# Transposing a per-pair attention tile by DMA instead of on TensorE, with the add on VectorE and a longer lag of the MLP

## The chip, the cores and the metric

One Trainium2 chip, one core. The metric is device time in microseconds (us) of one execution. The kernel before takes 316 to 318 us. One slot below means one step of the main loop: one head's scores for 128 keys. A pair is two heads and has 12 slots; a batch is four pairs and has 48 slots.

## The reference

```python
# q, k, v: [4, 8, 768, 64]; block-sparse mask over 24 blocks of 32
scores = q @ k.T / 8, masked; attn = softmax(scores); x = attn @ v     # -> x: [4, 768, 512]
xt = x.transpose(0, 2, 1)
h  = xt @ U @ V                              # low-rank mixer over the sequence, rank 32
u  = x + h.transpose(0, 2, 1)
out = u + relu(u @ w_ch1) @ w_ch2            # 512 -> 2048 -> 512
```

## The kernel before

For every pair of heads the kernel computes 12 score tiles (two matmuls of 384 columns each), takes their exponentials on ScalarE, multiplies them with v (`av`), casts the normalized result to fp16 (`xh`), and forms `uT`, the transposed input of the MLP: x transposed plus the mixer's product. The MLP of a batch runs as 56 steps (32 for the first layer, 24 for the second), which are dealt out over the slots of the next batch, so that TensorE always has work while ScalarE takes exponentials.

In the kernel before, `xh` is transposed on TensorE: six matmuls against the identity, accumulated in PSUM with the mixer product, and then one cast to SBUF by VectorE.

```python
    def ut(c):                                   # c = 0, 1: two halves of the sequence
        pu = psa([P, HS], FP32)                  # one of two PSUM buffers "pa"
        for j in range(3):
            nc.tensor.matmul(pu[:, j * P : (j + 1) * P], xh[:, 3 * c + j, :], id16,
                             start=(j == 0), stop=False, ...)
        nc.tensor.matmul(pu, bt.a16[:, ch], Vt[...], start=False, stop=True, ...)
        nc.vector.tensor_copy(out=bt.uT[hp][:, c * HS : (c + 1) * HS], in_=pu)

    return {1: [lambda: av(0)], 3: [lambda: av(1)], 5: [mix],
            6: [lambda: ut(0)], 7: [lambda: ut(1)]}   # slots after the pair's last score
```

q, k and v are loaded by DMA from the queue of SyncE (SP), cast by GpSimd into `qst` and `kst`, and, from pair 6 on, transposed by DMAs from the same queue that transpose on the way (crossbar DMA). Two staging buffers each are reused by every other pair. The w2 weights are loaded from GpSimd's queue near 51 us.

```python
    def load_qk(i): ...   # nc.sync.dma_start(ld <- q, k); nc.gpsimd.tensor_copy(qst[i % 2] <- ld)
    def front(i):   ...   # i >= 6: nc.sync.dma_start_transpose(aq <- qst), (ak <- kst)

    for i in range(NPAIR):
        if i + 2 < NPAIR:
            last = load_qk(i + 2)
            load_v(i + 2)
            ...
        if i + 1 < NPAIR and i + 1 >= NPE:
            front(i + 1)
        ...           # 12 slots: scores, delayed functions of the pair before, MLP steps
```

The softmax here doesn't subtract the row's maximum and nothing guards it: scores larger than these inputs give would overflow.

Of the kernel before, what the change touches and what calls it, by code (L numbers as in the profile page):

```python
# [10 lines left out]
FP16 = mybir.dt.float16  # L11
# [3 lines left out]
ALU = mybir.AluOpType  # L15

P = 128
# [3 lines left out]
def kernel(  # L21
# [14 lines left out]
    nc = tc.nc  # L36

    B, H, S, D = q.shape
    BLK = 32
    NB = S // BLK  # L40
    T = S // P
    HD = H * D
    HP = H // 2
# [4 lines left out]
    HS = S // 2  # L48
# [31 lines left out]
    wpool = ctx.enter_context(tc.tile_pool(name="wpool", bufs=1))  # L80
    ldpool = ctx.enter_context(tc.tile_pool(name="ldpool", bufs=2))
    augp = ctx.enter_context(tc.tile_pool(name="augp", bufs=3))
    epool = ctx.enter_context(tc.tile_pool(name="epool", bufs=20))
    xpool = ctx.enter_context(tc.tile_pool(name="xpool", bufs=2))
    upool = ctx.enter_context(tc.tile_pool(name="upool", bufs=2))
    tpool = ctx.enter_context(tc.tile_pool(name="tpool", bufs=18))
# [13 lines left out]
    def psa(shape, dtype):  # L100
        return psap.tile(shape, dtype, tag="pa", name="pa")
# [5 lines left out]
    id16 = eye[:, 0:P]  # L107
# [14 lines left out]
    def load_qk(i):  # L122
        b, hp = divmod(i, HP)
        last = None
        for src, st, nm in ((q, qst, "qld"), (k, kst, "kld")):
            ld = ldpool.tile([P, 2, T, D], FP32, tag="ld" + nm, name=nm)
            nc.sync.dma_start(
                out=ld,
                in_=src[b, 2 * hp : 2 * hp + 2].rearrange("h (p t) d -> p h t d", t=T),
            )  # L130
            dst = st[i % NST][:, :, :, 0:D]
            last = nc.gpsimd.tensor_copy(out=dst, in_=ld)  # L132
        return last

    def load_v(i):
        b, hp = divmod(i, HP)
        ld = ldpool.tile([P, 2, T, D], FP32, tag="ldv", name="vld")
        nc.sync.dma_start(
            out=ld,
            in_=v[b, 2 * hp : 2 * hp + 2].rearrange("h (p t) d -> p h t d", t=T),  # L140
        )
        nc.gpsimd.tensor_copy(out=vts[b % 2][:, 2 * hp : 2 * hp + 2, :, 0:D], in_=ld)
# [3 lines left out]
        out=sb[0:NB].rearrange("k z r w -> k (z r w)"),  # L146
        in_=sampled_blocks.bitcast(I32).rearrange("z r -> (z r)")[None, :].broadcast_to(
            [NB, NB * 6]
        ),
# [3 lines left out]
    for h, eng in ((0, nc.sync), (1, nc.sync)):  # L153
        for src, nm in ((q, "qld"), (k, "kld")):
            if h == 0:
                lds[nm] = ldpool.tile([P, 2, T, D], FP32, tag="ld" + nm, name=nm)
            eng.dma_start(  # L157
                out=lds[nm][:, h], in_=src[0, h].rearrange("(p t) d -> p t d", t=T)
# [22 lines left out]
    for r in range(3):  # L181
        nc.vector.scalar_tensor_tensor(
            out=a01[0:NB], in0=sb[0:NB, :, r, 0], scalar=iota,
            in1=prev, op0=ALU.is_equal, op1=ALU.max,
# [3 lines left out]
        out=bias[0:NB, 0:NB], in0=a01[0:NB],  # L188
# [3 lines left out]
    for t in range(T):  # L192
        nc.tensor.matmul(
            pb[:, t, :], ohT[:, t * P : (t + 1) * P], bias[0:NB, :],
            start=True, stop=True,
# [10 lines left out]
    def load_mix():  # L206
        uld = ldpool.tile([P, T, R], FP32, tag="ldu", name="uld", bufs=1)
        nc.sync.dma_start(out=uld, in_=moe_U.rearrange("(p t) r -> p t r", t=T))
        vld = ldpool.tile([P, S], FP32, tag="ldvv", name="vvld", bufs=1)
        nc.sync.dma_start(out=vld[0:R, :], in_=moe_V)  # L210
        nc.gpsimd.tensor_copy(out=Ut[:, :, 0:R], in_=uld)
        nc.gpsimd.tensor_copy(
            out=Vt[0:R, :, :], in_=vld[0:R, :].rearrange("r (p t) -> r t p", t=T)
        )

    def load_w1(cs):
        for cc in cs:
            nc.gpsimd.dma_start(
                out=w1t[:, cc, :], in_=moe_w_ch1[cc * P : (cc + 1) * P, :]
            )  # L220

    def load_w2(js):
        for j in js:
            nc.gpsimd.dma_start(
                out=w2t[:, j : j + 4, :],
                in_=moe_w_ch2[j * P : (j + 4) * P, :].rearrange(
                    "(j p) d -> p j d", p=P
                ),
            )
# [3 lines left out]
    NPAIR = B * HP  # L233
# [51 lines left out]
    def pair_tail(i, bt, ests):  # L285
        b, hp = divmod(i, HP)
        vt = vts[b % 2]
        xh = xpool.tile([P, T, P], FP16, tag="xh", name="xh", bufs=3)
        ch = slice(hp * P, (hp + 1) * P)

        def av(c):
            pav = psa([P, 3, 2, D + 1], FP32)
            for h in range(2):
                for j in range(3):
                    sc = 3 * c + j
                    for g in range(T):
                        nc.tensor.matmul(  # L297
                            pav[:, j, h, :],
                            ests[h][g][:, sc * P : (sc + 1) * P],
                            vt[:, 2 * hp + h, g, 0 : D + 1],  # L300
                            start=(g == 0), stop=(g == T - 1),
                        )
            rcp = misc.tile([P, 3, 2], FP32, tag="rcp", name="rcp")
            nc.vector.reciprocal(out=rcp, in_=pav[:, :, :, D])  # L304
            xs = bt.xf[:, 3 * c : 3 * c + 3, ch]
            nc.vector.tensor_tensor(  # L306
                out=xs.rearrange("p j (h d) -> p j h d", h=2),
                in0=pav[:, :, :, 0:D],
                in1=rcp[:, :, :, None].broadcast_to([P, 3, 2, D]),
                op=ALU.mult,  # L310
            )
            nc.vector.tensor_copy(out=xh[:, 3 * c : 3 * c + 3, :], in_=xs)  # L312

        def mix():
            pa = psa([P, P], FP32)
            for sc in range(T):
                nc.tensor.matmul(  # L317
                    pa, Ut[:, sc, :], xh[:, sc, :], start=(sc == 0), stop=(sc == T - 1)
                )
            nc.vector.tensor_copy(out=bt.a16[:, ch], in_=pa)  # L320

        def ut(c):
            pu = psa([P, HS], FP32)
            for j in range(3):
                nc.tensor.matmul(  # L325
                    pu[:, j * P : (j + 1) * P], xh[:, 3 * c + j, :], id16,
                    start=(j == 0), stop=False, skip_group_check=True,
                )
            nc.tensor.matmul(  # L329
                pu,  # L330
                bt.a16[:, ch],
                Vt[:, 3 * c : 3 * c + 3, :].rearrange("r t p -> r (t p)"),
                start=False, stop=True, skip_group_check=True,
            )
            nc.vector.tensor_copy(out=bt.uT[hp][:, c * HS : (c + 1) * HS], in_=pu)

        return {
            1: [lambda: av(0)],
            3: [lambda: av(1)],
            5: [mix],  # L340
            6: [lambda: ut(0)],
            7: [lambda: ut(1)],
        }

# [50 lines left out]



    LAG = 8
    SLOTS = HP * 2 * T
    queue = []  # L400
    delayed = {}
    arrivals = {}
    slot = 0

    def run_delayed():
        for fn in delayed.pop(slot, ()):
            fn()
        queue.extend(arrivals.pop(slot, ()))
# [5 lines left out]
    for i in range(NPAIR):  # L414
        b, hp = divmod(i, HP)
        if hp == 0:
            bt = Batch()
            done, due = 0.0, 0.0
# [3 lines that stand above are left out]
            if i == 0:  # L422
                load_mix()
            with tc.issue_after(last.ins):
                if i == 0:
                    load_w1((0, 1))
                elif i == 1:
                    load_w1((2, 3))
                elif i == 4:
                    load_w2((0, 4, 8, 12))  # L430
        if i + 1 < NPAIR and i + 1 >= NPE:
            front(i + 1)
        ests = [[], []]
        for h in range(2):
            for g in range(T):
                ests[h].append(scores(i, h, g))
                run_delayed()
                n = slot % SLOTS
                if b > 0:
                    left = SLOTS - n  # L440
                    rest = [c for c, _ in queue]
                    if arrivals:
                        rest += [c for c, _ in arrivals_all]
                    keep = LAG if b + 1 < B else 0
                    due += sum(rest[: len(rest) - keep]) / left
                    while queue and done + queue[0][0] / 2 <= due:
                        c, fn = queue.pop(0)
                        fn()
                        done += c
                if i + 1 < NPE and (h, g) == (1, 2):  # L450
                    front(i + 1)
                slot += 1
        for d, fns in pair_tail(i, bt, ests).items():
            delayed.setdefault(slot + d, []).extend(fns)
        if hp == HP - 1:
            arrivals_all = mlp_steps(b, bt)
            arrivals[slot + 8] = arrivals_all
    while delayed:
        run_delayed()
        if queue:  # L460
# [37 lines left out]
```

## Time and profile before

The lines are from the page of the kernel before: busy time of each engine, then, for 40 equal slices of the span (7.9 us each), the busy share of TensorE, the clock granted to it and the busy share of the DMA engines, in tenths.

```profile
PE 304.8 (97%) x2840; PEld 188.6 (60%) x2840; DVE 128.6 (41%) x265; ACT 179.7 (57%) x261; POOL 48.0 (15%) x66
...
PE   6899999999999999999999999999999999999994
...
PEclk9999999999999999999999999999999999999999
DMA  7999887999797873551406160160001001000111
```

TensorE is busy from end to end at full clock. DMA is busy for seven tenths of the time or more in each of the first 15 slices, that is for batch 0 and most of batch 1 (to about 118 us), and less after that. The chain of work that ended last says the same:

```profile
PE 86%; ACT 7%; DMA 2%; DVE 1%; issue 1%; POOL 1%; SPq 1%; ACTq 0%
```

The groups of instructions (busy us, mean ns of one) show the identity matmuls, and a VectorE operation of the kind that the change adds:

```profile
L325 PE MATMUL pa<-eye,xh 128*128 128x128 f16 x96 | 10.6, 219 | 0.0
L306 DVE TENSOR_TENSOR xf<-pa,rcp 128x384 f32<-128x384 f32 x32 | 17.8, 557 | 1.1
```

The 219 ns is the modelled duration of one matmul, which overlaps its neighbours. What one costs is seen from start times in the timeline (start us, modelled duration, instruction, how many):

```profile
140.10 0.33 PE L325 MATMUL pa<-eye,xh 128*128 128x128 f16 x3
140.26 0.33 PE L329 MATMUL pa<-Vt,a_1986 128*128 128x384 f16 x1
140.43 0.33 PE L354 MATMUL pm<-uT_951,w1t 128*128 128x384 f16 x1
```

Three identity matmuls take from 140.10 to 140.26 us, 54 ns each. The queue of SP, again as a timeline, shows what a crossbar transpose (of q or k, twice the size of xh) costs to issue, once while DMA is full and once while it is not:

```profile
55.76 5.94 SPq L251 DMA_TRANSPOSE aq<-qst_99  x1
61.76 7.94 SPq L251 DMA_TRANSPOSE ak<-kst_101  x1
...
129.56 1.42 SPq L251 DMA_TRANSPOSE aq<-qst_100  x1
131.03 1.83 SPq L251 DMA_TRANSPOSE ak<-kst_102  x1
```

### The profile page before, as it was taken

How to read it: one execution, taken by the hardware profiler on the slowest of the kernel's cores; microseconds unless marked ns; L12 is line 12 of the kernel's file. 1: busy time of each engine (PE TensorE's matmuls, PEld its weight loads, DVE VectorE, ACT ScalarE, POOL GpSimd, SP SyncE). 2: the span in 40 equal slices, each digit the busy share in tenths (PEclk: the TensorE clock that was granted, in tenths of full speed). 3: DMA queues.
4: the chain of work that ended last, by engine and by line, in shares of the span. 5: the costliest groups of instructions: out<-in, count | busy, mean ns of one | idle time of the engine just before them, and what ended most of it. 6: DMA issues, size and time to landing. Idle time of an engine off the chain costs nothing.

```text
span 314.6 us, 6818 instructions
## 1 busy us (share of the span) xinstructions
PE 304.8 (97%) x2840; PEld 188.6 (60%) x2840; DVE 128.6 (41%) x265; ACT 179.7 (57%) x261; POOL 48.0 (15%) x66
## 2 busy tenths in 40 slices
PE   6899999999999999999999999999999999999994
PEld 3577666676756555666756555576665656565441
DVE  3455566545342424453533423454441334543111
ACT  4799988477756554767664554766655352332000
POOL 3871357004212311010202000000000000000000
PEclk9999999999999999999999999999999999999999
DMA  7999887999797873551406160160001001000111
GB/s 222 344 293 247 310 245 207 216 182 192 194 202 204 237 150 130 112 124 31 71 2 135 52 150 36 50 85 2 0 2 67 35 35 68 2 0 1 69 67 67
DMA packets 51031, 38.05 MB, mean 121 GB/s; under 512 B 32744, under 2 KB 47384, under 8 KB 51000
## 3 DMA queue, kind: packets, MB, share of 16 engines
q1 hardware_dynamic: 48240, 33.37, 40.3%
q0 software_dynamic: 2688, 4.19, 7.4%
q8 instruction: 22, 0.36, 0.5%
q14 instruction: 9, 0.07, 0.1%
q10 hardware_dynamic: 72, 0.05, 0.1%
HBM read 27.64 MB, written 6.29 MB: 108 GB/s over the span
## 4 chain that ended last, share of the span: by engine, by line
PE 86%; ACT 7%; DMA 2%; DVE 1%; issue 1%; POOL 1%; SPq 1%; ACTq 0%
PE pm L373 23%; PE pm L354 23%; PE psc L262 17%; PE pa L297 9%; ACT est L268 7%; PE pa L354 3%; PE pa L373 3%; PE pa L317 2%; DMA vld<-in_v_dram 2%; PE pa L329 2%; PE pm L371 1%; PE pa L325 1%; PE pa L245 1%; SPq L157 1%; DVE xf L306 0%
## 5 line engine op out<-in xcount | busy, mean ns | idle before, releaser
L268 ACT ACTIVATE est<-psc 128x768 f16<-128x768 f32 x192 | 150.7, 811 | 68.8 <-PE psc L262 68.1
L262 PE MATMUL psc<-aq,ak 128*128 128x384 f16 x384 | 93.5, 325 | 0.8 <-ACT est L268 0.2
L373 PE MATMUL pm<-w2t,tT 128*128 128x512 f16 x336 | 84.2, 379 | 0.0
L354 PEld LDWEIGHTS <-w1t 128*128 128x128 f16 x512 | 49.0, 98 | 31.0 <-issue 1.4
L373 PEld LDWEIGHTS <-tT 128*128 128x128 f16 x384 | 36.6, 98 | 36.2
L262 PEld LDWEIGHTS <-ak 128*128 128x128 f16 x384 | 36.6, 98 | 28.6 <-issue 1.8
L362 ACT ACTIVATE tT<-pm 128x384 f16<-128x384 f32 x64 | 31.3, 489 | 35.7 <-PE pm L354 19.7
L297 PEld LDWEIGHTS <-est 128*128 128x128 f16 x1152 | 43.0, 97 | 6.6
L364 DVE TENSOR_SCALAR tT<-pm 128x384 f16<-128x384 f32 x48 | 26.8, 557 | 33.4 <-PE pm L354 32.0
L381 DVE TENSOR_TENSOR of<-xf,pm 128x512 f32<-128x512 f32 x21 | 14.4, 685 | 34.1 <-PE pm L373 34.1
L304 DVE RECIPROCAL rcp<-pa 128x6 f32<-128x6 f32 x32 | 6.3, 195 | 52.6 <-PE pa L297 52.6
L297 PE MATMUL pa<-vt_97,est 128*128 128x65 f16 x576 | 24.0, 193 | 0.0
L297 PE MATMUL pa<-vt_98,est 128*128 128x65 f16 x576 | 20.7, 193 | 0.0
L306 DVE TENSOR_TENSOR xf<-pa,rcp 128x384 f32<-128x384 f32 x32 | 17.8, 557 | 1.1
L312 DVE CAST xh<-xf 128x384 f16<-128x384 f32 x32 | 17.6, 551 | 0.9
L364 DVE TENSOR_SCALAR tT<-pa 128x384 f16<-128x384 f32 x16 | 8.9, 557 | 11.3 <-PE pa L354 11.3
L132 POOL CAST qst_100<-qld 128x768 f16<-128x768 f32 x8 | 6.6, 828 | 41.5 <-DMA aq<-qst_100 34.7
L132 POOL CAST qst_99<-qld 128x768 f16<-128x768 f32 x7 | 5.8, 828 | 44.9 <-DMA aq<-qst_99 44.6
L373 PE MATMUL pa<-w2t,tT 128*128 128x512 f16 x48 | 10.8, 379 | 0.0
L325 PE MATMUL pa<-eye,xh 128*128 128x128 f16 x96 | 10.6, 219 | 0.0
L354 PE MATMUL pm<-uT_213,w1t 128*128 128x384 f16 x32 | 10.4, 325 | 0.1
L354 PE MATMUL pm<-uT_1987,w1t 128*128 128x384 f16 x32 | 10.4, 326 | 0.1
(101 smaller groups left out, 304.5 us busy)
## 6 DMA issues: line engine op xcount, KB each, us to landing
vld<-in_v_dram SPq DMA_DIRECT2D x16, 384.0 KB, 4.5
out_dram<-of SPq DMA_DIRECT2D x24, 256.0 KB, 2.0
qld<-in_q_dram SPq DMA_DIRECT2D x15, 384.0 KB, 3.4
kld<-in_k_dram SPq DMA_DIRECT2D x15, 384.0 KB, 6.2
w1t<-in_moe_w_ch_dram POOLq DMA_DIRECT2D x4, 512.0 KB, 8.7
w2t<-in_moe_w_ch_dram POOLq DMA_DIRECT2D x4, 512.0 KB, 13.3
qld<-in_q_dram SPq DMA_DIRECT2D x2, 192.0 KB, 3.4
kld<-in_k_dram SPq DMA_DIRECT2D x2, 192.0 KB, 3.5
```

Of the source, the lines that this page charges most:

```text
L132: last = nc.gpsimd.tensor_copy(out=dst, in_=ld)
L262: nc.tensor.matmul(psc[:, c, 0:HS], kT[:, h, g * P : (g + 1) * P], qT[:, h, c * HS : (c + 1) * HS], start=True, stop=True,)
L268: nc.scalar.activation(out=est.rearrange("k (c n) -> k c n", c=2), in_=psc[:, :, 0:HS], func=AF.Exp, scale=0.125,)
L297: nc.tensor.matmul(pav[:, j, h, :], ests[h][g][:, sc * P : (sc + 1) * P], vt[:, 2 * hp + h, g, 0 : D + 1], start=(g == 0), stop=(g == T - 1),)
L306: nc.vector.tensor_tensor(out=xs.rearrange("p j (h d) -> p j h d", h=2), in0=pav[:, :, :, 0:D], in1=rcp[:, :, :, None].broadcast_to([P, 3, ...
L312: nc.vector.tensor_copy(out=xh[:, 3 * c : 3 * c + 3, :], in_=xs)
L325: nc.tensor.matmul(pu[:, j * P : (j + 1) * P], xh[:, 3 * c + j, :], id16, start=(j == 0), stop=False, skip_group_check=True,)
L354: nc.tensor.matmul(pt, w1t[:, cc, jj * P : (jj + 1) * P], bt.uT[cc][:, c * HS : (c + 1) * HS], start=(cc == 0), stop=(cc == NCC - 1),)
L362: nc.scalar.activation(out=dst, in_=pt, func=AF.Relu)
L364: nc.vector.tensor_scalar_max(out=dst, in0=pt, scalar1=0.0)
L373: nc.tensor.matmul(hold[sc], bt.tT[jj][:, sc * P : (sc + 1) * P], w2t[:, jj, :], start=False, stop=(jj == NJJ - 1),)
L381: nc.vector.tensor_add(out=of, in0=bt.xf[:, sc, :], in1=hold[sc])
```

## The change

For pairs 4 to 14 the six identity matmuls go. `xh` is transposed into a new tile `xT` by a crossbar DMA that is issued from SP after the second attention product, and VectorE adds it to the mixer product in place of the cast. The additions move from slots 6 and 7 to slots 8 and 9 to give the DMA time. The MLP of batches 1 and 2 therefore starts at slot 10 rather than 8, and four more steps of the MLP before it are kept back to fill those slots. The pool of exponentials shrinks from 20 to 18 buffers to make room for `xT`.

```diff
-    epool = ctx.enter_context(tc.tile_pool(name="epool", bufs=20))
+    epool = ctx.enter_context(tc.tile_pool(name="epool", bufs=18))
...
+        xbar = HP <= i < NPAIR - 1
+        xT = xpool.tile([P, T, P], FP16, tag="xT", name="xT") if xbar else None
+
+        def turn():
+            nc.sync.dma_start_transpose(xT, xh.rearrange("p t c -> p (t c)"))
+
         def ut(c):
             pu = psa([P, HS], FP32)
-            for j in range(3):
+            if not xbar:                      # the same three matmuls
...
-            nc.vector.tensor_copy(out=bt.uT[hp][:, c * HS : (c + 1) * HS], in_=pu)
+            if xbar:
+                nc.vector.tensor_tensor(out=dst, in0=pu, in1=xT[...], op=ALU.add)
+            else:
+                nc.vector.tensor_copy(out=dst, in_=pu)
+
+        if xbar:
+            return {
+                1: [lambda: av(0)],
+                3: [lambda: av(1), turn],
+                5: [mix],
+                8: [lambda: ut(0)],
+                9: [lambda: ut(1)],
+            }
...
-    LAG = 8
+    LAG = 12
...
-            arrivals[slot + 8] = arrivals_all
+            arrivals[slot + (10 if 0 < b < B - 1 else 8)] = arrivals_all
```

More of the change, by code (lines that the diff above doesn't have):

```diff
@@ L320, in mix @@
             nc.vector.tensor_copy(out=bt.a16[:, ch], in_=pa)
+        xbar = HP <= i < NPAIR - 1
+        xT = xpool.tile([P, T, P], FP16, tag="xT", name="xT") if xbar else None
+        def turn():
+            nc.sync.dma_start_transpose(xT, xh.rearrange("p t c -> p (t c)"))
         def ut(c):
             pu = psa([P, HS], FP32)
-            for j in range(3):
-                nc.tensor.matmul(
-                    pu[:, j * P : (j + 1) * P], xh[:, 3 * c + j, :], id16,
-                    start=(j == 0), stop=False, skip_group_check=True,
-                )
+            if not xbar:
+                for j in range(3):
+                    nc.tensor.matmul(
+                        pu[:, j * P : (j + 1) * P], xh[:, 3 * c + j, :], id16,
+                        start=(j == 0), stop=False, skip_group_check=True,
+                    )
             nc.tensor.matmul(
@@ L332, in ut @@
                 Vt[:, 3 * c : 3 * c + 3, :].rearrange("r t p -> r (t p)"),
-                start=False, stop=True, skip_group_check=True,
+                start=xbar, stop=True, skip_group_check=True,
             )
-            nc.vector.tensor_copy(out=bt.uT[hp][:, c * HS : (c + 1) * HS], in_=pu)
+            dst = bt.uT[hp][:, c * HS : (c + 1) * HS]
+            if xbar:
+                nc.vector.tensor_tensor(
+                    out=dst, in0=pu,
+                    in1=xT[:, 3 * c : 3 * c + 3, :].rearrange("c t p -> c (t p)"),
+                    op=ALU.add,
+                )
+            else:
[8 more added lines that the diff above has]
+            }
         return {
```

## The prediction

> **What bounds the kernel.** TensorE. The page gives PE 97% busy; busy can hide slack, since ends are modelled, so I took start times from the timeline. From 54 us to the end (ScalarE paces the earlier part) matmuls start back to back: 163 ns per 384 columns, 216 ns per 512, 54 ns per 128, 32 ns per 65. Starts minus these sums leave under 0.5 us per 10 us, except about 1.5 us near 265 us. The granted clock is 1.00. In the chain of waits PE is 86%. VectorE (41%) and ScalarE (57%) have room.
>
> **Removed.** Eleven pairs (4 to 14) each lose six 128-column matmuls, the transposes of xh by the identity: 66 of 96. The group list says 219 ns each and 10.6 us busy for all 96, but neither is the cost: in the timeline three run from 140.10 to 140.26 us, 54 ns each. The Trainium skill ("TensorE: Matmul & The Clock Gate", Part 4) gives about 275 to 390 ns for a PE transpose; that is latency, and this trace's pipelined 54 ns decides. 66 x 54 ns = 3.6 us, all in PE-bound stages, so all on the chain.
>
> **Added.** (a) On VectorE, an add of PSUM and fp16 SBUF for a cast: the cast takes 558 ns, tensor-tensor operations of the same 128x384 shape 557 ns. Free. (b) Eleven crossbar transposes of 128x768 fp16. Those of q and k are twice as large: 1.4 us of issue on SP, 3.8 us at least and 4.7 us in the median to landing, 15.1 us at worst. Estimate for half: 0.7 us issue, about 3 us landing. (c) The addition comes five slots (about 7 us) after the second attention product; xT is ready 1.3 us plus landing after it. Enough where DMA is free (after 125 us: 10 to 40% busy), tight from 54 to 125 us, where DMA is 88% busy. Pair 5 is worst: its xh is cast at 88 us, while SP issues q/k transposes until 92 us. If the new one queues behind them, VectorE waits perhaps 3 us in order; with two PSUM buffers for the MLP some of that reaches PE. I charge 0.5 to 1 us in all.
>
> **Moved.** Twelve lagged steps in place of eight carry four w2 steps (0.86 us each) out of batch 1's stage into later ones. PE is saturated in all, so this saves nothing; it bridges the two slots by which the next MLP starts later (ten slots at about 2100 columns against twelve steps of 2048: no gap). Exponential buffers 20 to 18: never the releaser of a long wait; no effect expected.
>
> **Prediction.** 316.7 - 3.6 + 0.6 = 313.7 us, range 311.6 to 316.6. Faster by over 2%: 0.04; within 2%: 0.92; slower by over 2%: 0.04.
>
> **What would show it right or wrong.** Identity matmuls on xh fall from 96 to 30. Start spacing of other matmuls from 54 us on is unchanged. The uT additions take 0.55 to 0.6 us. VectorE waits for the xT DMA at most once or twice, near 75 to 97 us, and PE shows gaps only there. The stage up to 54 us and the tail from about 263 us keep their lengths.
>
> **What would make it wrong.** If xT lands late in most pairs, in-order VectorE holds both PSUM pools and TensorE stalls: each 1 us late, times eleven, would eat the gain. If the extra DMA delays q/k loads in batch 1's stage, scores start late. If the buffer count reorders the first stage, up to 1 us either way. More than 4 us gained would mean that weight loads or PSUM waits cost more than the timeline's spacing shows.

## The result, and the profile after

The changed kernel takes 330.41 us (median of four runs, 328.92 to 331.66) against 317.48 us. It is slower: the ratio is 1.0409, with a 95% interval of 1.0338 to 1.0479. The prediction said 313.7 us.

The lines of the page of the changed kernel that answer to those of before:

```profile
PE 303.7 (93%) x2774; PEld 185.7 (57%) x2774; DVE 128.3 (39%) x265; ACT 180.2 (55%) x261; POOL 48.1 (15%) x66
...
PE   7899999993089999999999999999999999899995
...
PEclk9999999998559999999999999999999999999999
DMA  7999888998847587566423625361001121000111
...
PE 78%; DMA 8%; ACT 6%; POOL 2%; DVE 2%; SPq 1%; issue 1%; ACTq 0%; POOLq 0%; DVEq 0%
```

66 matmuls are gone (2840 to 2774). But in the tenth and eleventh slices (8.2 us each, from 74 to 90 us) TensorE is mostly idle, and its granted clock falls to about half in the eleventh and is no higher in the twelfth, where it works again. The chain of waits now holds 8% DMA. The list of waits names one event (who waited for whom; us in total, times, longest):

```profile
DVE uT_951 L344 <- DMA xT<-xh: 16.9, 1, 16.9
PE pm L377 <- DVE tT L387: 15.0, 1, 15.0
DVE uT_953 L344 <- DMA xT<-xh: 3.0, 1, 3.0
```

uT_951 is pair 4, the first pair that uses the crossbar. TensorE's timeline around it:

```profile
76.11 0.33 PE L377 MATMUL pm<-uT_216,w1t 128*128 128x384 f16 x1
76.27 0.49 PE L262 MATMUL psc<-aq,ak 128*128 128x384 f16 x2
91.75 0.48 PE L377 MATMUL pm<-uT_213,w1t 128*128 128x384 f16 x1 [14.99 <-DVE tT L387]
92.03 0.52 PE L377 MATMUL pm<-uT_214,w1t 128*128 128x384 f16 x1
```

TensorE waits 15 us for a PSUM buffer of the MLP, which VectorE must empty (tT, line 387). VectorE's timeline says why it does not:

```profile
70.13 0.55 DVE L312 CAST xh<-xf 128x384 f16<-128x384 f32 x1
...
73.22 0.56 DVE L387 TENSOR_SCALAR tT<-pm 128x384 f16<-128x384 f32 x1 [1.33 <-PE pm L377]
90.67 0.56 DVE L344 TENSOR_TENSOR uT_951<-pa,xT 128x384 f16<-128x384 f32 x1 [16.90 <-DMA xT<-xh]
```

VectorE runs in order. Its next instruction is the addition of pair 4's `xT`, so the emptying of the MLP's buffers stands behind it. The data for that transpose, `xh`, was complete at 70.68 us (the cast at 70.13 plus 0.55). SP's queue shows when the transpose was issued:

```profile
61.36 8.39 SPq L251 DMA_TRANSPOSE ak<-kst_101  x1
72.27 0.37 SPq L127 DMA_DIRECT2D qld<-in_q_dram  x1
74.91 0.37 SPq L127 DMA_DIRECT2D kld<-in_k_dram  x1
75.68 0.37 SPq L127 DMA_DIRECT2D qld<-in_q_dram  x1
76.45 0.37 SPq L127 DMA_DIRECT2D kld<-in_k_dram  x1
76.91 1.84 SPq L251 DMA_TRANSPOSE aq<-qst_100  x1
78.88 3.12 SPq L251 DMA_TRANSPOSE ak<-kst_102  x1
83.40 0.37 SPq L127 DMA_DIRECT2D qld<-in_q_dram  x1
84.75 0.38 SPq L127 DMA_DIRECT2D kld<-in_k_dram  x1
85.52 0.37 SPq L138 DMA_DIRECT2D vld<-in_v_dram  x1
85.95 1.23 SPq L326 DMA_TRANSPOSE xT<-xh  x1
```

The transpose was ready to go at 70.68 us and was issued at 85.95 us, behind nine other commands. Once issued it took 4.7 us to land. The order of the queue is set when the kernel is built. With the built program's own numbers it reads as follows (place in SP's queue, command, and, added here, the pair that it serves); the trace has the commands in the same order:

```
40 qld_1739  pair 9       44 aq_1510   pair 7
41 kld_1742  pair 9       45 ak_1511   pair 7
42 qld_1959  pair 10      46 qld_2194  pair 11
43 kld_1962  pair 10      47 kld_2197  pair 11
48 vld_2993  pair 14      49 xT_1250   pair 4
```

In the program, pair 4's transpose stands ahead of all nine: it belongs to pair 5's slot 3, while they come at the starts of pairs 6 to 12. The build had moved them ahead. Most of them wait for something: the loads for GpSimd's casts to free their buffers, the casts for the transposes of an earlier pair to have read `qst` and `kst`. In the kernel before this queue was just as long and as slow, and nobody was harmed, because nothing in it was urgent. The Trainium skill ("DMA: Bandwidth & Descriptors", section "Anatomy of one DMA — SWDGE (gpsimd) path") says that DMA engines do not wait on semaphores: any such wait happens on the issuing sequencer, before dispatch. The section follows a DMA of GpSimd; this trace shows the same for SP: from 69 to 86 us SP waited seven times for GpSimd's casts, 7.9 us in all, and what stood behind waited too. Of the 15.3 us, 7.6 us are the issue times of the nine commands (the lines above), and most of the rest is these waits.

A second cost follows the first. These lines give the busy time of each engine in four stretches of the changed kernel (stretch, length, busy us and instructions of PE, PEld, DVE, ACT and POOL, granted clock, DMA share, GB/s):

```profile
76.60:80.00 3.40, 0.16 (x1) 0.00 (x0) 0.00 (x0) 1.06 (x2) 0.00 (x0) 0.96 0.97 302
80.00:91.70 11.70, 0.00 (x0) 0.00 (x0) 1.02 (x3) 0.00 (x0) 2.43 (x3) 0.50 0.78 194
91.70:95.00 3.30, 3.25 (x11) 1.52 (x11) 1.02 (x2) 0.81 (x1) 0.00 (x0) 0.50 0.00 0
...
97.00:100.00 3.00, 3.00 (x49) 2.28 (x48) 1.86 (x4) 1.69 (x3) 1.04 (x2) 1.00 0.88 150
```

The granted clock falls to one half after about 3 us of idling (the last matmul's modelled end is at 76.8 us, and a mean of 0.96 up to 80.00 us puts the fall near 79.7), and it is still one half when TensorE has work again. From 91.75 to 96.81 us, 16 matmuls of 384 columns take 5.06 us where 16 x 163 ns = 2.6 us would do: 2.5 us more. The Trainium skill ("TensorE: Matmul & The Clock Gate", Part 1, "What's actually happening") gives half clock after at least one idle window of about 3.4 us, and full clock again after a busy window of that length; the 3 us and 5.1 us here are of that order.

The spans differ by 328.0 - 314.6 = 13.4 us. The stall (15.15 us, start to start, beyond the matmuls' own time) and the slow restart (2.5 us) make 17.6 us. So the rest of the changed kernel is 4.2 us shorter; the 66 removed matmuls would be 3.6 us of it.

### The profile page after: what moved, and what is told of

It reads as the page before. It is cut to its first block, busy times and chain, and to the rows that moved or that the text cites. A ratio compares the mean times of both kernels' runs of the same rounds, so it can differ in the third digit from the quotient of the medians.

```text
span 328.0 us, 6715 instructions
## 1 busy us (share of the span) xinstructions
PE 303.7 (93%) x2774; PEld 185.7 (57%) x2774; DVE 128.3 (39%) x265; ACT 180.2 (55%) x261; POOL 48.1 (15%) x66
## 4 chain that ended last, share of the span: by engine, by line
PE 78%; DMA 8%; ACT 6%; POOL 2%; DVE 2%; SPq 1%; issue 1%; ACTq 0%; POOLq 0%; DVEq 0%
PE pm L396 22%; PE pm L377 20%; PE psc L262 15%; PE pa L297 8%; ACT est L268 6%; DMA ak<-kst_101 4%; PE pa L377 3%; PE pa L396 3%; PE pa L317 2%; DMA ak<-kst_102 1%; DMA vld<-in_v_dram 1%; DMA xT<-xh 1%; PE pa L336 1%; PE pm L394 1%; PE pa L245 1%
## 5 line engine op out<-in xcount | busy, mean ns | idle before, releaser
L377 PE MATMUL pm<-uT_213,w1t 128*128 128x384 f16 x32 | 11.0, 342 | 15.1 <-DVE tT L387 15.0
L377 PE MATMUL pm<-uT_215,w1t 128*128 128x384 f16 x32 | 11.0, 344 | 0.0
L377 PE MATMUL pm<-uT_214,w1t 128*128 128x384 f16 x32 | 11.0, 344 | 0.0
L377 PE MATMUL pm<-uT_216,w1t 128*128 128x384 f16 x32 | 11.0, 342 | 0.0
```

Source lines behind the costliest of these rows:

```text
L377: nc.tensor.matmul(pt, w1t[:, cc, jj * P : (jj + 1) * P], bt.uT[cc][:, c * HS : (c + 1) * HS], start=(cc == 0), stop=(cc == NCC - 1),)
```

## The experiments

Theory S: nothing but the late issue costs time. Rival D: the added transposes overload DMA, so they land late whatever the order. Rival L: the longer lag, the later start of the MLP or the smaller pool costs the time. All eleven runs gave correct results.

### e1_pair4_pe: pair 4 back on TensorE

```diff
-        xbar = HP <= i < NPAIR - 1
+        xbar = HP < i < NPAIR - 1
```

> Pair 4 alone goes back to its six identity matmuls on TensorE; pairs 5 to 14 keep the crossbar. Theory S (the whole loss is one wait: pair 4's transpose stood behind nine older commands in SP's in-order queue, and TensorE then restarted at half clock): 330.4 - 15.2 - 2.4 + 0.3 = about 313 us, no TensorE gap over 1 us between 54 us and the tail, granted clock 1.00. Rival D (the added transposes overload DMA while q/k/v and w2 are loaded, so the first one is late whichever it is): pair 5 now waits in its place, over 318 us. Rival L (the lag of twelve, the later start of the MLP or the smaller exponential pool cost the time): stays near 330 us.

Measured: 323.62 us against 316.45 us, ratio 1.0209 (1.0149 to 1.0269). My theory as written, with pair 4 alone to blame, missed by 10 us. The list of waits shows that the delay went to the next pair:

```profile
DVE uT L344 <- DMA xT<-xh: 11.1, 1, 11.1
PE pa L297 <- DVE uT L344: 6.1, 1, 6.1
```

Pair 5's `xh` was complete at 85.7 us and its transpose was issued at 95.69 us, 10 us later, again behind loads and transposes of later pairs. TensorE stood still for 6.2 us and then lost 2.2 us at half clock, which together are about the 8.4 us by which this run's span exceeds that of e2_order (319.2 against 310.8 us). In the changed kernel pair 5 had been spared (its transpose left 3.1 us after its data); I take it that the queue drained during the 15 us stall of pair 4. So the fault is not of one pair; but this run alone cannot tell theory S from rival D.

### e2_order: the same instructions, another order on SP

`issue_after(x)` puts what its block issues on x's engine behind x in the queue, without waiting for x to finish.

```diff
+            turns[i] = nc.sync.dma_start_transpose(xT, xh...)       # in turn()
...
+    def behind_turn(i):
+        return tc.issue_after(turns[i].ins) if i in turns else nullcontext()
...
-            last = load_qk(i + 2)
-            load_v(i + 2)
+            with behind_turn(i - 2):
+                last = load_qk(i + 2)
+                load_v(i + 2)
...
-            front(i + 1)
+            with behind_turn(i - 2):
+                front(i + 1)
```

> The same instructions as the changed kernel; only SP's order differs: the loads and q/k transposes of a pair are put behind the xh transpose of the pair four before it (issue order only). Theory S: pair 4's transpose is issued within 2 us of its cast (near 71 us instead of 86), VectorE waits for it under 3 us, 312 to 314 us. Rival D: it is issued early but lands late all the same, or scores start late because loads were held back: over 318 us. Rival L: near 330 us.

Measured: 312.83 us, ratio to the kernel before 0.9889 (0.9849 to 0.9929): 1.1% faster, and the interval excludes 1. SP's queue and VectorE's timeline around pair 4:

```profile
71.13 1.21 SPq L326 DMA_TRANSPOSE xT<-xh  x1
72.39 0.58 SPq L127 DMA_DIRECT2D qld<-in_q_dram  x1
```

```profile
70.55 0.55 DVE L312 CAST xh<-xf 128x384 f16<-128x384 f32 x1
...
75.10 0.56 DVE L346 TENSOR_TENSOR uT<-pa,xT 128x384 f16<-128x384 f32 x1 [0.90 <-PE pa L338]
```

The transpose now leaves 0.03 us after the cast has ended, and VectorE waits for TensorE, not for the DMA; in the whole run it waits for no `xT`. The granted clock of the profiled execution is 1.000. The number and size of the transposes are those of the changed kernel, so rival D falls. A new order of one queue is enough to remove the whole loss.

### e3_no_xbar: only the lag, the later start and the pool

```diff
-        xbar = HP <= i < NPAIR - 1
+        xbar = False
```

> All pairs transpose on TensorE again (two slots earlier, as before), but the lag stays twelve, the MLP of batches 1 and 2 still starts ten slots late and the exponential pool still has 18 buffers. Theory S: these three cost nothing, 315.5 to 318 us, as the kernel before. Rival L: over 325 us.

Measured: 316.75 us against 316.45 us, ratio 1.0004 (0.9965 to 1.0043). Rival L falls.

### e4_late_add: the additions twelve slots later, three pairs of each batch

```diff
+        late = 12 if hp < HP - 1 else 0
...
-                8: [lambda: ut(0)],
-                9: [lambda: ut(1)],
+                8 + late: [lambda: ut(0)],
+                9 + late: [lambda: ut(1)],
```

> The changed kernel, but for the first three pairs of each batch the mixer product and the addition of xT come twelve slots later (20 and 21 instead of 8 and 9); uT is not needed before the next batch's stage. Theory S: pair 4's transpose is still issued near 86 us and lands near 91 us, but VectorE reaches its addition only at about 92 us, so the wait is under 2 us and the time 312 to 315 us. If the lateness also hurts by another way than VectorE's in-order wait, the time stays over 320 us.

Measured: 316.23 us, ratio 1.0003 (0.9956 to 1.0049). The big wait is gone (VectorE's longest wait for `xT` is 2.0 us), but the time is above the 312 to 315 us expected. The timeline shows a fault of my edit: twelve slots are one pair, so a late pair's additions fall on the slots of the next pair's. Near 123 us four of them want the two PSUM buffers and TensorE waits 1.6 us; and pair 14's additions slip past the last score into the tail. By start times TensorE loses 1.8 us there, 0.9 us in the tail, and 0.8 us near 94 us, where VectorE's 2.0 us wait does reach it: 3.5 us more than in e2_order, which is about the distance between the two medians (3.4 us).

### e5_w2_early: the bad order kept, the w2 loads earlier

In batch 1's stage the transposes of pair 6 took 16.4 and 12.6 us to land in the changed kernel, while w2 was being loaded, against 3.8 to 5.5 us elsewhere. Was that why the queue was slow?

```diff
-                elif i == 4:
+                elif i == 2:
                     load_w2((0, 4, 8, 12))
```

> The changed kernel with its bad SP order kept, but the four loads of w2 are issued two pairs earlier (near 34 us instead of 51). If the queue ahead of pair 4's transpose was slow because the q/k transposes of pair 6 shared the DMA engines with w2 (15 and 12 us to land, against 3.8 to 5 elsewhere), those now land in about 5 us, the queue drains sooner and pair 4's transpose is issued by about 76 us: the wait shrinks to 0 to 5 us, 312 to 318 us. If order alone matters and w2 does not, it stays near 330 us. Early w2 may cost 1 to 2 us in the first stage, where DMA is full.

Measured: 325.18 us against 316.54 us, ratio 1.0248 (1.0188 to 1.0307). It lies between my two outcomes. SP's queue in this run:

```profile
60.99 2.47 SPq L251 DMA_TRANSPOSE aq<-qst  x1
63.51 2.74 SPq L251 DMA_TRANSPOSE ak<-kst  x1
...
80.62 1.23 SPq L326 DMA_TRANSPOSE xT<-xh  x1
```

The transposes of pair 6 no longer crawl: issuing both takes 5.2 us instead of 14.8. But w2 now delayed the v loads ahead of them, so they start 6 us later, and the rest of the queue still takes its time. Pair 4's transpose is issued at 80.62 us, 8 us after its data; VectorE waits 9.8 us and TensorE about 8. So w2's traffic made the queue worse (the wait before issue falls from 15.3 to 8.0 us, though the queue also starts later here), but without it the order alone still costs more than the change can earn.

### e6_both: the order of e2, and the identity matmuls too

`xT` is written and not read; the cast and all identity matmuls are back. Otherwise this is e2_order.

```diff
-            if not xbar:
+            if True:                       # identity matmuls for every pair
...
-            if xbar:
+            if False:                      # cast, no addition
```

> As e2_order with the same DMA transposes, lag, pools and SP order, but all identity matmuls are done as well and xT is not read. If e2_order's gain over the kernel before is the 66 removed matmuls (54 ns each), it is given back in full: 316 to 317.5 us. If the gain came from the new SP order or the lag, it stays near 313 us.

Measured: 316.03 us against 316.54 us, ratio 0.9958 (0.9906 to 1.0011). With the matmuls back the gain goes: the interval holds 1, and the median lies 3.2 us above e2_order's (of the job before; the kernel before differed by 0.1 us between the two). The ratios of the two runs overlap at their edges, but all four executions here (315.87 to 316.28 us) lie above all four of e2_order (312.34 to 314.15). So the gain comes from the removed matmuls, not from the new order. The 0.4% that is left is mostly spread of the kernel before: three of its seven executions in this job show a granted clock of 0.992 or 0.993 and take 318.1 to 318.8 us, and the other four (0.998 to 1.000) take 316.1 to 316.5 us, within 0.7 us of all of e6_both's.

### e7_order_lag8: the order of e2 with eight lagged steps

```diff
-    LAG = 12
+    LAG = 8
```

> As e2_order with eight lagged steps in place of twelve. If the lag bridges the two slots by which the next MLP starts later, batches 2 and 3 now begin with two slots each with no MLP work, where ScalarE's 0.75 us per slot paces TensorE: 1 to 2 us in all, 313.8 to 315 us. If the lag does nothing, within 0.5 us of e2_order.

Measured: 314.91 us, ratio 0.992 (0.9865 to 0.9976). The interval overlaps that of e2_order, so it was timed again (below).

### e8_late_b1: the bad order kept, only pairs 4 to 6 added ten slots later

This is e4's edit with `late = 10 if b == 1 and hp < HP - 1 else 0`, so that no two pairs collide and none reaches the tail.

> The changed kernel with the bad SP order, and the additions of pairs 4, 5 and 6 alone ten slots later (18 and 19), so that they collide with no other pair's additions and none reaches the tail, as those of e4_late_add did. Theory: nothing but VectorE's in-order wait costs time, so 312.5 to 314.5 us; e4_late_add's other 3 us were its own collisions (1.6 us at 123 us) and tail. If it stays at 316 us, the late transposes cost in another way.

Measured: 312.25 us, ratio 0.9851 (0.98 to 0.9902). Here pair 4's transpose is issued as late as in the changed kernel (86.90 us), and the addition comes late too:

```profile
91.69 0.56 DVE L344 TENSOR_TENSOR uT<-pa,xT 128x384 f16<-128x384 f32 x1 [3.62 <-DMA xT<-xh]
```

VectorE waits 3.6 us, and TensorE shows no gap there at all; it starts the next matmul after 0.86 us, four times the 216 ns of 512 columns:

```profile
91.58 1.03 PE L397 MATMUL pm<-w2t,tT 128*128 128x512 f16 x4
92.44 0.49 PE L262 MATMUL psc<-aq,ak 128*128 128x384 f16 x2
```

So a late transpose does no harm by itself. The harm is that an in-order VectorE meets the addition before the data. This is a second version that beats both kernels, without touching the queue.

### f1_order, f2_order_lag8, f3_order_slots67: what the later slots and the lag are worth

f1 and f2 are e2 and e7 again, with more rounds. f3 is f1 with the slots, the start of the MLP and the lag of the kernel before:

```diff
-                8: [lambda: ut(0)],
-                9: [lambda: ut(1)],
+                6: [lambda: ut(0)],
+                7: [lambda: ut(1)],
...
-    LAG = 12
+    LAG = 8
...
-            arrivals[slot + (10 if 0 < b < B - 1 else 8)] = arrivals_all
+            arrivals[slot + 8] = arrivals_all
```

> The same kernel as e2_order, timed again with more rounds beside the next two, which ask what its lag and its later slots are worth: 312.3 to 313.5 us.

> The same kernel as e7_order_lag8 (eight lagged steps, additions at slots 8 and 9). In the first job it lay 0.3% above e2_order, within the interval. If the lag bridges a gap: 0.8 to 2 us above f1_order. If it does nothing: within 0.5 us.

> SP order as in f1_order, but the additions at slots 6 and 7, the next MLP at slot 8 and eight lagged steps, all as in the kernel before. xT is ready about 1.3 us (products to cast) plus 2.7 us (landing) after the second attention product, three slots are 3.5 to 4.5 us: if that is too short, VectorE waits about 0.5 us per pair and 1 to 3 us reach TensorE (313.5 to 316 us); if it is enough, the later slots and the longer lag buy nothing, within 0.5 us of f1_order.

| run | median us | ratio to before | 95% interval |
|---|---|---|---|
| f1_order | 312.25 | 0.9885 | 0.9857 to 0.9912 |
| f2_order_lag8 | 313.76 | 0.9917 | 0.9898 to 0.9936 |
| f3_order_slots67 | 312.69 | 0.9897 | 0.9868 to 0.9926 |

The kernel before had a median of 316.38 us in this job. Eight steps with the later slots cost about 1 us by the ratios (1.5 us by the medians), as the bridging argument says, though the intervals overlap. The trace of f2 shows where: eleven pauses of TensorE, of 0.05 to 0.20 us each and 1.4 us in all by start times, at 125 to 129 us and 195 to 204 us, where the MLPs of batches 1 and 2 start. e7, the same kernel, has the same eleven; f1 has none there. One of them (two matmuls of 384 columns take 0.53 us from start to start instead of 0.33):

```profile
126.58 0.49 PE L262 MATMUL psc<-aq,ak 128*128 128x384 f16 x2
127.11 2.20 PE L379 MATMUL pm<-uT,w1t 128*128 128x384 f16 x12
```

So with the later slots the lag does bridge a gap, as the prediction said. f3 is not to be told from f1: with the queue in order, the later slots and the longer lag together buy nothing that these runs resolve. VectorE does wait for `xT` in f3:

```profile
DVE uT L346 <- DMA xT<-xh: 6.7, 4, 2.1
```

Four waits, 6.7 us together, the longest 2.1 us; the time shows none of it. TensorE's start times show no gap at these waits: short waits of VectorE are absorbed here.

## Why the prediction was wrong, point by point

- **TensorE bounds the kernel: right.** e6_both and e2_order differ by the identity matmuls, and 3.2 us of time come back with them.
- **Removed, 66 x 54 ns = 3.6 us: right in size.** e2_order and f1_order are 1.1% faster than the kernel before, 3.5 to 3.6 us; the profile shows 66 matmuls less.
- **Added (a), VectorE's addition is free: right.** It takes 547 to 558 ns; I said 550 to 600.
- **Added (b), the transpose itself: nearly right.** Landing took 2.7 to 4.7 us, 3.0 in the median, where I estimated 3. Issue took 1.2 us where I estimated 0.7: half the data did not halve the issue time (1.4 us).
- **Added (c), the step that failed:** "xT is ready 1.3 us plus landing after it". I counted the time from issue to landing and left out the time from ready to issue. It was 15.3 us for pair 4 (and 10 us for pair 5 in e1, where VectorE waited 11.1 us against the 3 I had named for pair 5). I saw the danger for pair 5 alone, because there SP was visibly issuing transposes at 88 to 92 us; I read the queue's busy time as its load, and took the gaps between commands for free time. They were not free: SP stood in them, with its next command waiting for GpSimd. Nor did I ask where the build would put the new command: it stands behind nine that the program writes after it. I charged 0.5 to 1 us; the stall was 15.15 us, and the restart at half clock, which I did not count at all, 2.5 us. The way in which lateness reaches TensorE, through VectorE's order and the PSUM buffers, was in the prediction; it was feared only as about 1 us in each of eleven pairs, not as one long wait.
- **Moved: right as far as it went.** e3_no_xbar shows that lag, start and pool alone cost nothing, and f2's pauses that the lag bridges the later start.
- **What would show it wrong:** I said that VectorE would wait at most twice, between 75 and 97 us, and that TensorE's gaps would lie only there. That held for the large gap (76 to 92 us); a second VectorE wait of 3.0 us, for pair 6, came at 120 to 123 us, and TensorE shows no gap there. What I did not foresee was that a single wait could hold nearly five times the gain. The first stage and the tail kept their lengths (the matmuls of the first MLP start to run back to back at 54.6 us against 54.8, and the end follows the last attention products by 51.6 us against 51.8).

## What to carry to other kernels

When you move work to a DMA queue, cost the queue as well as the transfer: list which commands stand before the new one, in the order as built and not as written, and what each of them waits for. A queue of prefetches that is late without harm becomes harmful once something urgent stands in it. Put the prefetches behind the urgent command (e2, f3), or let its consumer come so late that lateness doesn't matter (e8); and remember that an in-order consumer passes its wait on to work that had nothing to do with it.

## What the Trainium skill lacked or had wrong

- "DMA: Bandwidth & Descriptors" gives no issue or landing time on this chip for a crossbar transpose of this size from SBUF to SBUF. The changed kernel shows, for 128x768 fp16, 1.2 us of SP and 2.7 to 4.7 us to landing (3.0 in the median; 6.3 at most in any run, in e8); for twice that, 1.4 to 2.1 us of SP after 140 us, where DMA was light, 3.8 us at least to landing, and up to 8.4 us and 16.4 us while w2 was loading.
- The same page states that waits are served on the issuing sequencer, but its rule "Overlap DMA with compute" (Rules for kernel authors) says only to issue early and wait late. It lacks the warning that prefetches issued early can hold an urgent command in the same queue: 15.3 us here, and 17.6 us of time.
- "TensorE: Matmul & The Clock Gate", Part 4, gives 275 to 390 ns for a 128x128 transpose on TensorE in its transpose mode, and does not say what a transpose costs in a stream of other matmuls. Here the transposes were plain fp16 matmuls against the identity, each with its own weight load, and cost 54 ns each (140.10 to 140.26 us for three), which decides whether moving a transpose off TensorE can pay. For plain matmuls of 128 columns the page has 55 to 56 ns back to back (Part 1), which this agrees with, and about 81 ns where each loads its weights (Part 2, "Back-to-back issue gap"), which it does not.
